# A fused retention, ELU and maxout kernel: the loads and the order of work of its first eight chunks

## The chip, the cores and the metric

The kernel runs on one core of one Trainium2 chip. The metric is the device time of one execution in microseconds (us), median over runs. TensorE (PE) multiplies matrices, VectorE (DVE) and ScalarE (ACT) work element by element, GpSimd (POOL) does a little, SyncE (SP) issues transfers. Each engine executes its own instructions in their written order and waits on semaphores for the others.

## The reference

Three layers stand one behind the other; only what matters is shown.

```
# 1 retention, B=4, H=8, S=768, D=64, gamma[h] = 1 - 2**(-5-h)
state = gamma * state + k[t] outer v[t];   y[t] = q[t] @ state / 8
x = y as (3072 tokens, 512)
# 2 ELU layer, d_ff = 2048
h = x @ w_in;  g = where(h > 0, h, exp(min(h, 0)) - 1);  x = g @ w_out
# 3 maxout layer, three experts of 768
h = max(x @ w1, x @ w2, x @ w3);  out = h @ w_out
```

The weights of layers 2 and 3 arrive in float64.

## The kernel before

Retention is worked in 24 chunks of 128 tokens (6 a batch entry). For a chunk `c`, `load(c)` brings 1 MB to a tile `x`: queries and keys transposed (L98 twice, the queries by halves; L100, the keys), then keys and values by token (L106). `scores` multiplies queries by keys on PE (L154, tile `sc`); `prep` scales the queries by `qdec` (DVE, tile `qd`) and the keys by a column of `cols` (ACT, 8 instructions at L136, tile `kd`), or both into a tile `spare` in an odd chunk; `mask` multiplies the scores by the decay table `dmask` (DVE, L166, tile `a`). `update` forms keys times values (PE, L182, tile `up`) and adds it to the decayed state (DVE, L189 and L192); `mix` makes the outputs from the old state (PE, L205) and from masked scores and values (PE, L209), both into `xo`, and casts them (ACT, L217, `xh`); `rest` keeps what the cast lost (DVE, L222, `xl`). The state makes this a chain over the chunks.

Four chunks are a block of 512 tokens for the ELU layer. `h1(b, f)` is 12 matmuls of block `b` with a 128-column piece `f` of `w_in` (L339), then exp, Relu, a max and a split on ACT and DVE (L346 to L352); `o1(b, f, ...)` is 12 matmuls with the same piece of `w_out` into four accumulators (L371); `x2_out` copies these out (L390, L392). Each product is made of three passes over high and low parts. A half of a piece's float64 words comes in by `load_half` (L244, tile `raw`, 512 KB, two buffers) and is turned into high and low float32 parts by `cv_bits`, `cv_rest`, `cv_high`, `cv_low`: six instructions on DVE and two on ACT; `cv_high` issues the load of the half after next.

PE, DVE, ACT and SP execute in the order in which the program is written. So the start of the program, up to the eight chunks, two `h1` and two `o1`, is an order made by hand: `begin(c)` is scores, prep, mask; `end(c)` is update, then mix. `junk(k)` is `k` matmuls on a tile of zeros. Behind that a loop over `(b, f)` runs one `h1` and one `o1` after the other with one conversion each, the later chunks between them, and a third part does the maxout layer.

Of the kernel before, what the change touches and what calls it, by code (L numbers as in the profile page):

```python
# [7 lines left out]
F32 = mybir.dt.float32  # L8
# [32 lines left out]
def kernel(ctx: ExitStack, tc: tile.TileContext, qkv0, qkv, wa, wb, dmask, qdec, cols, out):  # L41
# [8 lines left out]
    xpool = ctx.enter_context(tc.tile_pool(name="x", bufs=2))  # L50
    ps_acc = ctx.enter_context(tc.tile_pool(name="ps_acc", bufs=4, space=bass.MemoryType.PSUM))
    ps_h = ctx.enter_context(tc.tile_pool(name="ps_h", bufs=4, space=bass.MemoryType.PSUM))
    const = one.enter_context(tc.tile_pool(name="const", bufs=1))
    wpool = one.enter_context(tc.tile_pool(name="w", bufs=KFF - NRING))
    stage = one.enter_context(tc.tile_pool(name="stage", bufs=NSTAGE))
    ld = one.enter_context(tc.tile_pool(name="ld", bufs=2))
    at = one.enter_context(tc.tile_pool(name="at", bufs=1))
    dpool = one.enter_context(tc.tile_pool(name="dec", bufs=2))


    dmask_sb = const.tile([P, H, P], F32, name="dmask_sb")
    qdec_sb = const.tile([P, NPAIR, P], F32, name="qdec_sb")
    cols_sb = const.tile([P, 32], F32, name="cols_sb")[:, :H + NPAIR]
    state = [const.tile([P, NPAIR, D], F32, name=f"state{i}") for i in range(2)]
    x2d = dram.tile([KDM, P, NT], F32, name="x2d")
    kept = {(f, c): dram.tile([P, 2 * 512], F32, name=f"kept{f}_{c}") for f in range(RES, KFF) for c in range(2)}
    opd = [dram.tile([P, SETW], F32, name=f"opd{j}") for j in range(NE * KF2 // 2)]
# [10 lines left out]
    def load(c, part=None):  # L78


        if c >= NCHUNK:
            return

        early = c < EARLY
        src = qkv0 if early else qkv
        if part != 1:
            if c in raw_t:
                return
            if c < EARLY + 3:
                x = wpool.tile([P, NPAIR, 4, P], F32, tag="w", name="x")  # L90
            else:
                x = ld.tile([P, NPAIR, 4, P], F32, tag="r", name="x")
            raw_t[c] = x
            for r in range(2):
                h = slice(r * D, (r + 1) * D)
                for s in range(1 if early else 2):
                    cc = slice(s * 2 * P + r * P, s * 2 * P + (r + 1) * P)
                    nc.sync.dma_start(out=x[h, :, s, :], in_=src[c, :, h, cc].rearrange("p d t -> d p t"))  # L98
            if early:
                nc.sync.dma_start(  # L100
                    out=x[:, :, 1, :], in_=src[c, :, :, 2 * P:3 * P].rearrange("p t n -> t p n")
                )
        if part != 0:
            x = raw_t[c]
            o = 3 * P if early else 4 * P
            nc.sync.dma_start(  # L106
                out=x[:, :, 2:4, :].rearrange("t p s n -> t p (s n)"),
                in_=src[c, :, :, o:].rearrange("p t n -> t p n"),
            )
# [84 lines left out]
    def mix(c, pool, tag, then=None):  # L194
        v = raw_t[c][:, :, 3, :].rearrange("t p (r d) -> t p r d", r=2)
        qd = st_t[c][0]
        a = a_t.pop(c)
        xo = xo_t[c] = pool.tile([P, NPAIR, P], F32, tag=tag, name="xo")
        first = True
        if c % NCH != 0:  # L200
            old = state[1 - c % 2]
            for p in range(NPAIR):
                for r in range(2):
                    h = slice(r * D, (r + 1) * D)
                    nc.tensor.matmul(xo[h, p, :], old[h, p, :], qd[h, p, :], start=p == 0, stop=False)  # L205
            first = False
        for p in range(NPAIR):
            for r in range(2):
                nc.tensor.matmul(  # L209
                    xo[r * D:(r + 1) * D, p, :], v[:, p, r, :], a[:, r, p, :],  # L210
                    start=first and p == 0, stop=p == NPAIR - 1,
                )
        if then:
            then(c, pool, tag)
        del raw_t[c], st_t[c]
        b, t0 = divmod(c * P, BLK)
        nc.scalar.copy(x_t[b][0][:, :, t0:t0 + P], xo)  # L217

    def rest(c):
        b, t0 = divmod(c * P, BLK)  # L220
        xh, xl = x_t[b]
        nc.vector.tensor_tensor(  # L222
            out=xl[:, :, t0:t0 + P], in0=xo_t.pop(c), in1=f32(xh[:, :, t0:t0 + P]), op=ALU.subtract
        )
# [9 lines left out]
    def load_half(n):  # L234
        if n < len(keys):
            key = keys[n]
            if key[0] == "a":
                src, c = wa[key[1]], key[2]
            elif key[0] == "b":
                src, c = wb[2 * (2 * key[1] + key[3]) + key[2] // 2], key[2] % 2  # L240
            else:
                src, c = wb[2 * key[1] + 1], 1
            r = stage.tile([P, 512, 2], I32, tag="raw", name="raw")
            nc.sync.dma_start(  # L244
                out=r.rearrange("p n w -> p (n w)"), in_=src[:, c * 512:(c + 1) * 512].bitcast(I32)
            )
            half.append(r)
# [26 lines left out]
    def cv_bits(n):  # L274
        if n >= len(keys):
            return
        t = dpool.tile([P, 512], I32, tag="t", name="t")
        m = dpool.tile([P, 512], F32, tag="m", name="m")
        tmp[n] = (t, m)
        nc.vector.tensor_scalar(  # L280
            out=t, in0=half[n][:, :, 1], scalar1=0x7FFFFE00, scalar2=None, op0=ALU.bitwise_and
        )
        nc.scalar.activation(t, t, ACTF.Relu, scale=8.0, bias=-896.0 * 2 ** 23)  # L283

    def cv_rest(n):
        if n >= len(keys):
            return
        m = tmp[n][1]
        lo, hi = half[n][:, :, 0].bitcast(U32), half[n][:, :, 1]
        nc.vector.tensor_scalar(out=m.bitcast(I32), in0=hi, scalar1=0x1FF, scalar2=None, op0=ALU.bitwise_and)  # L290
        nc.vector.scalar_tensor_tensor(
            out=m, in0=lo, scalar=2.0 ** -32, in1=m.bitcast(I32), op0=ALU.mult, op1=ALU.add
        )
# [28 lines left out]
    def new_x(b):  # L322
        x_t[b] = (
            xpool.tile([P, KDM, BLK], F32R, tag="xh", name="xh"),
            xpool.tile([P, KDM, BLK], F32R, tag="xl", name="xl"),
        )
# [32 lines left out]
    def o1(b, f, f0, f1):  # L359
        g = g_t.pop((b, f))  # L360
        w = w_t[f, 1]
        if f == f0:
            acc_t[b] = [ps_acc.tile([P, BLK], F32, tag="acc", name="acc") for _ in range(KDM)]
        order = [[(1, 0), (0, 0)], [(0, 1)]]
        if fresh(b, f):
            order = [[p] for p in FRESH]
        first, final = order[0][0], order[-1][-1]
        for passes in order:
            for m in range(KDM):
                for p in passes:  # L370
                    nc.tensor.matmul(  # L371
                        acc_t[b][m], w[:, p[0], m * P:(m + 1) * P], g[p[1]],
                        start=f == f0 and p == first, stop=f == f1 - 1 and p == final,
                    )
# [125 lines left out]
    ctx.enter_context(tc.manual_schedule(engines={mybir.EngineType.SP}))  # L500
    ctx.enter_context(tc.manual_schedule(engines={mybir.EngineType.PE}))
    ctx.enter_context(tc.manual_schedule(engines={mybir.EngineType.DVE, mybir.EngineType.Activation}))
    load(0, 0)
    nc.sync.dma_start(out=cols_sb, in_=cols)
    nc.sync.dma_start(out=dmask_sb, in_=dmask)
    load(0, 1)
    load(1, 0)
    load(1, 1)
    nc.sync.dma_start(out=qdec_sb, in_=qdec)
    load(2)  # L510
    load(3)
    load_half(0)
    load_half(1)
    load(4)
    load(5)
    new_x(0)
    new_x(1)

# [4 lines left out]
    def junk(k):  # L523
        o = ps_h.tile([P, BLK], F32, tag="h", name="junk")
        for i in range(k):
            nc.tensor.matmul(o, zero[:, 0:P], zero, start=i == 0, stop=i == k - 1)  # L526

    def begin(c, pool=ps_h, tag="h"):
        scores(c, pool, tag)
        prep(c)  # L530
        mask(c)

    def end(c):
        update(c, ps_h, "h")
        mix(c, ps_h, "h")

    junk(15)
    begin(0, ps_acc, "acc")
    end(0)
    junk(12)  # L540
    rest(0)
    begin(1, ps_acc, "acc")
    for c in range(1, CB):
        if c + 1 < CB:
            begin(c + 1, ps_acc, "acc")
        end(c)
        if c < 3:
            rest(c)
            junk(5)
    cv_bits(0)  # L550
    cv_rest(0)
    rest(CB - 1)
    cv_high(0)
    load(6)
    cv_bits(1)
    cv_low(0)
    cv_rest(1)
    begin(4, ps_h, "h")
    h1(0, 0, [(cv_high, 1)])
    end(4)  # L560
    cv_low(1)
    begin(5, ps_h, "h")
    rest(4)
    o1(0, 0, 0, 2)
    cv_bits(2)
    cv_rest(2)
    end(5)
    cv_high(2)
    load(7)
    rest(5)  # L570
    cv_low(2)
    begin(6, ps_h, "h")
    h1(0, 1, [], [(cv_bits, 3)])
    end(6)
    begin(7, ps_h, "h")
    rest(6)
    cv_rest(3)
    cv_high(3)
    end(7)
    cv_low(3)  # L580
    o1(0, 1, 0, 2)
    cv_bits(4)
    rest(7)
    cv_rest(4)
    h1(1, 0, [(cv_high, 4)], [(cv_bits, 5)])
    x2_out(0, 0, 2, True)
    cv_low(4)
    cv_rest(5)
    n = 5
# [376 lines left out]
```

## Time and profile before

| | |
|---|---|
| median of 3 runs | 1018.7 us (1017.85 to 1019.39) |
| profiled execution, its own time | 1019.52 us |
| its span | 1017.7 us |
| PE busy | 999.9 us (98%) |
| DVE, ACT busy | 690.5 us (68%), 353.3 us (35%) |

The span is the profiled part of the execution; 1.8 us lie around it. Busy PE includes the zeros and matmuls that wait inside the pipeline. The mean granted clock of PE is 0.995 of full speed.

### The profile page before, as it was taken

The numbers are of one execution on the slowest core, as the hardware profiler recorded it, in microseconds if no ns is written. First come the engines' busy times: TensorE is split into PE (matmuls) and PEld (weight loads), VectorE is DVE, ScalarE is ACT, GpSimd is POOL, SyncE is SP. The second block draws the span as 40 slices with busy tenths as digits, with TensorE's granted clock in tenths as the row PEclk, the third lists the DMA queues.
The fourth block names the chain that finished last, engine by engine and source line by source line (L and its number), as shares of the span: only waits on it lengthen the run. The fifth ranks groups of instructions, "written<-read, shape, count | busy, mean of one in ns | idle before, by whom it ended". The sixth has DMA issues, their size and how long they took to land.

```text
span 1017.7 us, 14387 instructions
## 1 busy us (share of the span) xinstructions
PE 999.9 (98%) x5690; PEld 853.6 (84%) x5693; DVE 690.5 (68%) x1189; ACT 353.3 (35%) x629; POOL 33.9 (3%) x31
## 2 busy tenths in 40 slices
PE   8989999999999999999999999999999999999998
PEld 4767888877788877888888788899899989999996
DVE  3869888985576776677765653678648836874771
ACT  3446555532344444444434543411301221130110
POOL 0000000020000100000100000000000000000000
PEclk8999999999999999999999999999999999999999
DMA  9423236794736783677437725994246045304701
GB/s 282 139 87 121 86 106 206 228 289 150 231 116 196 233 296 113 210 269 272 133 131 282 255 105 189 373 354 190 83 179 225 1 147 209 130 11 145 268 1 62
DMA packets 75315, 180.78 MB, mean 178 GB/s; under 512 B 5872, under 2 KB 42736, under 8 KB 71024
## 3 DMA queue, kind: packets, MB, share of 16 engines
q1 hardware_dynamic: 73520, 176.71, 50.5%
q10 hardware_dynamic: 1728, 3.15, 0.8%
q8 instruction: 45, 0.74, 0.3%
q14 instruction: 22, 0.18, 0.1%
HBM read 139.20 MB, written 40.63 MB: 177 GB/s over the span
## 4 chain that ended last, share of the span: by engine, by line
PE 91%; DVE 5%; ACT 2%; DMA 1%; issue 1%; SPq 0%; DVEq 0%; ACTq 0%
PE pp L682 26%; PE hp L339 25%; PE acc L371 24%; PE ac L734 9%; PE xo L209 2%; PE sc L154 2%; PE xo L205 2%; PE up L182 1%; DVE gl L352 1%; DVE e L348 1%; DMA x<-in_qkv 1%; PE junk L526 1%; DVE t L298 1%; ACT gh L349 0%; DVE part L388 0%
## 5 line engine op out<-in xcount | busy, mean ns | idle before, releaser
L682 PE MATMUL pp<-xs,op 128*128 128x384 f32 x1512 | 267.8, 334 | 0.0
L682 PEld LDWEIGHTS pp<-xs,op 128*128 128x128 f32 x1512 | 263.3, 188 | 3.0
L339 PE MATMUL hp<-xh,w 128*128 128x512 f32 x768 | 250.6, 397 | 4.4 <-DVE state L192 2.3
L371 PE MATMUL acc<-gh,w 128*128 128x512 f32 x768 | 196.3, 394 | 2.3 <-DVE part L392 1.7
L339 PEld LDWEIGHTS hp<-xh,w 128*128 128x128 f32 x768 | 143.9, 188 | 39.7 <-ACT w L301 2.5
L371 PEld LDWEIGHTS acc<-gh,w 128*128 128x128 f32 x768 | 143.5, 188 | 37.1 <-issue 2.4
L348 DVE SCALAR_TENSOR_TENSOR e<-e,hp 128x512 f32<-128x512 f32 x96 | 65.8, 685 | 124.1 <-ACT e L347 124.1
L339 PE MATMUL hp<-xl,w 128*128 128x512 f32 x384 | 143.2, 393 | 0.0
L734 PE MATMUL ac<-w,g 128*128 128x512 f32 x432 | 104.5, 391 | 0.0
L371 PE MATMUL acc<-gl,w 128*128 128x512 f32 x384 | 104.2, 393 | 0.0
L346 ACT ACTIVATE e<-hp 128x512 f32<-128x512 f32 x96 | 57.3, 597 | 117.3 <-PE hp L339 117.3
L734 PEld LDWEIGHTS ac<-w,g 128*128 128x128 f32 x432 | 80.6, 188 | 14.9
L349 ACT CAST gh<-e 128x512 fp32r<-128x512 f32 x96 | 59.6, 621 | 85.5 <-DVE e L348 85.5
L698 ACT COPY u<-pp 128x384 f32<-128x384 f32 x36 | 17.3, 480 | 201.5 <-PE pp L682 127.5
L371 PEld LDWEIGHTS acc<-gl,w 128*128 128x128 f32 x384 | 72.2, 188 | 16.4
L339 PEld LDWEIGHTS hp<-xl,w 128*128 128x128 f32 x384 | 72.3, 188 | 15.5
L352 DVE TENSOR_TENSOR gl<-e,gh 128x512 fp32r<-128x512 f32 x96 | 68.8, 717 | 19.6 <-ACT gh L349 16.9
L690 DVE TENSOR_TENSOR c<-pp,u 128x384 f32<-128x384 f32 x96 | 52.9, 553 | 36.4 <-PE pp L682 35.8
L347 ACT ACTIVATE e<-e 128x512 f32<-128x512 f32 x96 | 60.7, 632 | 3.1
L283 ACT ACTIVATE t<-t 128x512 int32<-128x512 int32 x56 | 35.4, 633 | 50.3 <-DVE t L280 50.3
L301 ACT CAST w<-t 128x512 fp32r<-128x512 f32 x56 | 34.8, 621 | 40.2 <-DVE t L298 38.6
L712 DVE TENSOR_TENSOR h<-h,c 128x768 f32<-128x768 f32 x48 | 45.9, 957 | 1.6
(70 smaller groups left out, 825.6 us busy)
## 6 DMA issues: line engine op xcount, KB each, us to landing
op<-opd SPq DMA_DIRECT2D x24, 1792.0 KB, 7.4
w<-kept SPq DMA_DIRECT2D x56, 512.0 KB, 6.0
raw<-in_wa SPq DMA_DIRECT2D x32, 512.0 KB, 3.7
x<-in_qkv SPq DMA_DIRECT2D x24, 512.0 KB, 6.0
raw<-in_wb SPq DMA_DIRECT2D x24, 512.0 KB, 4.3
x<-in_qkv SPq DMA_DIRECT2D x80, 128.0 KB, 4.8
opd<-w SPq DMA_DIRECT2D x9, 1024.0 KB, 6.9
kept<-w SPq DMA_DIRECT2D x14, 512.0 KB, 5.1
```

Source lines behind the costliest of these rows:

```text
L283: nc.scalar.activation(t, t, ACTF.Relu, scale=8.0, bias=-896.0 * 2 ** 23)
L339: nc.tensor.matmul(hp, w[:, pw, kk * P:(kk + 1) * P], x[px][:, kk, :], start=k == 0, stop=k == len(order) - 1,)
L346: nc.scalar.activation(e, hp, ACTF.Exp)
L347: nc.scalar.activation(e, e, ACTF.Relu, scale=-1.0, bias=1.0)
L348: nc.vector.scalar_tensor_tensor(out=e, in0=e, scalar=-1.0, in1=hp, op0=ALU.mult, op1=ALU.max)
L349: nc.scalar.copy(gh, e)
L352: nc.vector.tensor_tensor(out=gl, in0=e, in1=f32(gh), op=ALU.subtract)
L371: nc.tensor.matmul(acc_t[b][m], w[:, p[0], m * P:(m + 1) * P], g[p[1]], start=f == f0 and p == first, stop=f == f1 - 1 and p == final,)
L682: nc.tensor.matmul(o, ws[i][:, pw, kk * P:(kk + 1) * P], xs[i][:, px, kk, :], start=k == 0, stop=k == 5)
L690: nc.vector.tensor_tensor(out=out, in0=a, in1=c, op=ALU.add)
L712: nc.vector.tensor_tensor(out=h_t[s, p][i], in0=h_t[s, p][i], in1=c[i], op=ALU.max)
L734: nc.tensor.matmul(ac_t[s, m], g[:, px, m * P:(m + 1) * P], wo_t[f][:, pw, :], start=first and i == 0, stop=final and i == 2,)
```

## The change

The three tables (`cols`, `dmask`, `qdec`) are issued from ACT's queue and no longer from SP's, with one small `Exp` between them, in front of which the table load of ACT now stands. SP issues all eight early chunks without a pause, with the first two weight halves behind chunks 2 and 3; chunks 6 and 7 were issued behind `cv_high(0)` and `cv_high(2)`. `finish(c)` is mix, then update. In the first four chunks the scores of the next chunk come before the mix of this one, and in chunks 5 to 7 `prep` stands ahead of `scores`. The zeros go from 15, 12, 5 and 5 to 15, 10 and 4. `cv_bits(0)` and `cv_rest(0)` stand between the chunks. `x2_out` of the first group stands ahead of the next `h1`. The pool `const` is allocated behind the other pools, and `cols_sb` has 12 columns.

```diff
@@ pools
-    const = one.enter_context(tc.tile_pool(name="const", bufs=1))
     wpool = one.enter_context(tc.tile_pool(name="w", bufs=KFF - NRING))
...
     dpool = one.enter_context(tc.tile_pool(name="dec", bufs=2))
+    const = one.enter_context(tc.tile_pool(name="const", bufs=1))
-    cols_sb = const.tile([P, 32], F32, name="cols_sb")[:, :H + NPAIR]
+    cols_sb = const.tile([P, H + NPAIR], F32, name="cols_sb")
@@ start
-    load(0, 0)
-    nc.sync.dma_start(out=cols_sb, in_=cols)
-    nc.sync.dma_start(out=dmask_sb, in_=dmask)
-    load(0, 1)
-    load(1, 0)
-    load(1, 1)
-    nc.sync.dma_start(out=qdec_sb, in_=qdec)
+    warm = dpool.tile([P, 1], F32, tag="m", name="warm")
+    nc.vector.memset(warm, 0.0)
+    nc.scalar.dma_start(out=cols_sb, in_=cols)
+    nc.scalar.dma_start(out=dmask_sb, in_=dmask)
+    nc.scalar.activation(warm, warm, ACTF.Exp)
+    nc.scalar.dma_start(out=qdec_sb, in_=qdec)
+    load(0)
+    load(1)
     load(2)
+    load_half(0)
     load(3)
-    load_half(0)
     load_half(1)
     load(4)
     load(5)
+    load(6)
+    load(7)
+    def finish(c):
+        mix(c, ps_h, "h", update)
+
     junk(15)
     begin(0, ps_acc, "acc")
-    end(0)
-    junk(12)
+    junk(10)
+    begin(1, ps_acc, "acc")
+    finish(0)
     rest(0)
-    begin(1, ps_acc, "acc")
-    for c in range(1, CB):
-        if c + 1 < CB:
-            begin(c + 1, ps_acc, "acc")
-        end(c)
-        if c < 3:
-            rest(c)
-            junk(5)
+    junk(4)
+    begin(2, ps_acc, "acc")
+    finish(1)
+    rest(1)
     cv_bits(0)
+    begin(3, ps_acc, "acc")
+    finish(2)
+    rest(2)
     cv_rest(0)
-    rest(CB - 1)
     cv_high(0)
-    load(6)
+    finish(3)
+    rest(3)
     cv_bits(1)
...
     h1(0, 0, [(cv_high, 1)])
-    end(4)
+    prep(5)
+    finish(4)
     cv_low(1)
-    begin(5, ps_h, "h")
+    scores(5, ps_h, "h")
+    mask(5)
     rest(4)
+    prep(6)
     o1(0, 0, 0, 2)
...
     h1(0, 1, [], [(cv_bits, 3)])
-    end(6)
-    begin(7, ps_h, "h")
+    finish(6)
+    scores(7, ps_h, "h")
+    mask(7)
...
     o1(0, 1, 0, 2)
+    rest(7)
     cv_bits(4)
-    rest(7)
+    x2_out(0, 0, 2, True)
     cv_rest(4)
     h1(1, 0, [(cv_high, 4)], [(cv_bits, 5)])
-    x2_out(0, 0, 2, True)
```

On SP, at the start of the program, the queue of before reads so (`x_131`, `x_138`, `x_144` are chunks 0 to 2; `raw_424` is the third weight half, `x_426` chunk 6):

```order
L100 DMA x_131<-in_qkv0 128x4x128
L504 DMA cols_sb_92<-in_cols 128x12
L505 DMA dmask_sb_90<-in_dmask 128x1024
L106 DMA x_131<-in_qkv0 128x4x256
L98 DMA x_138<-in_qkv0 64x4x128 x2
L100 DMA x_138<-in_qkv0 128x4x128
L106 DMA x_138<-in_qkv0 128x4x256
L509 DMA qdec_sb_91<-in_qdec 128x512
...
L244 DMA raw_424<-in_wa 128x1024
L98 DMA x_426<-in_qkv0 64x4x128 x2
```

Of the change it reads (`x_137` is chunk 0, `x_147` chunk 2, `x_154` chunk 3, `x_176` chunk 7; `raw_152` and `raw_398` are the first and the third weight half):

```order
L100 DMA x_137<-in_qkv0 128x4x128
L106 DMA x_137<-in_qkv0 128x4x256
L98 DMA x_142<-in_qkv0 64x4x128 x2
...
L106 DMA x_147<-in_qkv0 128x4x256
L244 DMA raw_152<-in_wa 128x1024
L98 DMA x_154<-in_qkv0 64x4x128 x2
L100 DMA x_154<-in_qkv0 128x4x128
...
L106 DMA x_176<-in_qkv0 128x4x256
L244 DMA raw_398<-in_wa 128x1024
```

The tables have left the queue, the first weight half has moved ahead of chunk 3, and the third one has moved behind chunks 6 and 7.

On PE, chunks 1 to 3 stand so in before (`spare` is an odd chunk, `kd`, `qd` and `a` an even one; zeros left out):

```order
L154 MATMUL sc<-x 128x128 x16
L182 MATMUL up<-x,spare 64x64 x8
L205 MATMUL xo<-spare,state_93 64x128 x8
L209 MATMUL xo<-spare,x 64x128 x8
...
L154 MATMUL sc<-x 128x128 x8
L182 MATMUL up<-x,kd 64x64 x8
L205 MATMUL xo<-qd,state_94 64x128 x8
L209 MATMUL xo<-a,x 64x128 x8
```

and so in the change:

```order
L154 MATMUL sc<-x 128x128 x8
L205 MATMUL xo<-spare,state_92 64x128 x8
L209 MATMUL xo<-spare,x 64x128 x8
L182 MATMUL up<-x,spare 64x64 x8
L154 MATMUL sc<-x 128x128 x8
L205 MATMUL xo<-qd,state_93 64x128 x8
L209 MATMUL xo<-a,x 64x128 x8
L182 MATMUL up<-x,kd 64x64 x8
```

The state's products have moved behind the two products of the output, and between chunks 1 and 3 no zeros are left.

On DVE, behind the second `o1`, before:

```order
L280 TENSOR_SCALAR t<-raw 128x512
L222 TENSOR_TENSOR xl<-xo,xh 128x4x128
L290 TENSOR_SCALAR m<-raw 128x512
L291 SCALAR_TENSOR_TENSOR m<-raw,m 128x512
L348 SCALAR_TENSOR_TENSOR e<-e,hp 128x512
L298 SCALAR_TENSOR_TENSOR t<-raw,t 128x512
L352 TENSOR_TENSOR gl<-e,gh 128x512
L280 TENSOR_SCALAR t<-raw 128x512
L392 COPY part<-acc 128x512 x2
```

and in the change:

```order
L222 TENSOR_TENSOR xl<-xo,xh 128x4x128
L280 TENSOR_SCALAR t<-raw 128x512
L392 COPY part<-acc 128x512 x2
L290 TENSOR_SCALAR m<-raw 128x512
L291 SCALAR_TENSOR_TENSOR m<-raw,m 128x512
L348 SCALAR_TENSOR_TENSOR e<-e,hp 128x512
```

The copies of the accumulators have moved ahead of the whole elementwise work of `h1(1, 0)`. Behind the places that the diff touches, the order of every engine is the same as before.

## Rows read from the trace of the kernel before

**Rows 1.** Busy time by stretch: us of each engine, granted clock, DMA share, GB/s.

```profile
8.65:35.40 26.75, 21.44 (x260) 16.09 (x263) 14.64 (x28) 12.59 (x40) 0.00 (x0) 0.87 0.84 245
35.40:62.40 27.00, 24.02 (x244) 19.29 (x244) 23.16 (x43) 14.57 (x39) 0.00 (x0) 0.94 0.50 150
62.40:84.60 22.20, 20.07 (x87) 15.56 (x85) 15.90 (x30) 11.12 (x20) 0.00 (x0) 1.00 0.23 81
84.60:200.00 115.40, 115.40 (x495) 92.92 (x496) 103.09 (x187) 65.50 (x108) 2.35 (x2) 1.00 0.45 147
```

**Rows 2.** Chain that ended last, in order of time: start, us, what.

```profile
3.85 6.34 DMA x<-in_qkv
...
10.26 1.28 ACT L136
...
35.39 3.06 PE hp L339 x12
...
62.48 2.99 PE acc L371 x12
...
84.58 3.06 PE acc L371 x12
```

**Rows 3.** Who waited for whom, PE, first 104 us: total, times, longest.

```profile
PE acc L371 <- DVE part L392: 1.7, 1, 1.7
```

**Rows 4.** Busy time by stretch, as in Rows 1, two answers.

```profile
1.75:3.50 1.75, 1.75 (x6) 0.60 (x4) 0.00 (x0) 0.00 (x0) 0.00 (x0) 1.00 0.43 123
3.50:5.25 1.75, 1.75 (x6) 0.60 (x4) 0.00 (x0) 0.00 (x0) 0.00 (x0) 1.00 0.96 217
...
0.00:10.20 10.20, 7.43 (x31) 3.06 (x31) 1.56 (x3) 0.00 (x0) 0.20 (x4) 1.00 0.72 203
10.20:17.70 7.50, 5.41 (x37) 4.20 (x39) 1.66 (x3) 5.16 (x16) 0.00 (x0) 0.54 1.15 316
17.70:30.40 12.70, 12.60 (x173) 9.07 (x174) 8.08 (x16) 5.64 (x21) 0.00 (x0) 1.00 0.95 294
```

**Rows 5.** Timeline of SP's queue: start, us, line, operation, tiles.

```profile
2.83 0.50 SPq L504 DMA_DIRECT2D cols_sb<-in_cols  x1
3.37 0.43 SPq L505 DMA_DIRECT2D dmask_sb<-in_dmask  x1
...
48.59 1.26 SPq L98 DMA_DIRECT2D x<-in_qkv  x2
```

**Rows 6.** Chain that ended last, the steps of chunk 2 on PE.

```profile
25.13 1.09 PE sc L154 x16
26.22 0.61 PE up L182 x16
26.84 1.02 PE xo L205 x16
27.86 1.02 PE xo L209 x16
```

**Rows 7.** Timeline, DVE, and ACT behind the second `h1`: start, us, line, operation, tiles.

```profile
27.98 0.42 DVE L192 TENSOR_TENSOR state<-up,state 128x256 f32<-128x256 f32 x1
...
46.09 0.41 DVE L280 TENSOR_SCALAR t<-raw 128x512 int32<-128x512 int32 x1
...
51.96 0.60 ACT L346 ACTIVATE e<-hp 128x512 f32<-128x512 f32 x1 [1.22 <-PE hp L339]
...
53.98 0.62 ACT L349 CAST gh<-e 128x512 fp32r<-128x512 f32 x1 [0.75 <-DVE e L348]
```

**Rows 8.** Busy time by stretch, as in Rows 1: around PE's lower clock.

```profile
12.00:17.40 5.40, 5.07 (x35) 3.99 (x37) 1.36 (x3) 3.13 (x13) 0.00 (x0) 0.50 1.17 303
17.40:35.40 18.00, 16.33 (x226) 12.06 (x226) 11.99 (x24) 7.74 (x26) 0.00 (x0) 1.00 0.69 211
...
51.90:57.10 5.20, 2.77 (x50) 2.37 (x49) 3.16 (x6) 3.26 (x7) 0.00 (x0) 1.00 0.53 165
57.10:62.40 5.30, 5.30 (x48) 4.46 (x48) 5.03 (x11) 2.23 (x8) 0.00 (x0) 0.68 0.21 60
```

More of the change, by code (lines that the diff above doesn't have):

```diff
@@ L566 @@
     cv_rest(2)
-    end(5)
+    finish(5)
     cv_high(2)
-    load(7)
     rest(5)
     cv_low(2)
-    begin(6, ps_h, "h")
+    prep(7)
+    scores(6, ps_h, "h")
+    mask(6)
     h1(0, 1, [], [(cv_bits, 3)])
-    end(6)
-    begin(7, ps_h, "h")
+    finish(6)
+    scores(7, ps_h, "h")
+    mask(7)
     rest(6)
@@ L578 @@
     cv_high(3)
-    end(7)
+    finish(7)
     cv_low(3)
     o1(0, 1, 0, 2)
+    rest(7)
     cv_bits(4)
-    rest(7)
+    x2_out(0, 0, 2, True)
     cv_rest(4)
     h1(1, 0, [(cv_high, 4)], [(cv_bits, 5)])
-    x2_out(0, 0, 2, True)
     cv_low(4)
```

## The prediction

> **What bounds the kernel now.** I read the busy time by stretch first. From 84.6 us on PE has no idle time: 115.40 of 115.40 us up to 200, DVE 103.09 [rows 1]. The diff ends before that point and leaves the order behind it alone, so what the change is worth is how much earlier PE comes to this state, which is the `o1` that the chain of waits starts at 84.58 [rows 2]. Three stretches lie ahead of it, each with a limit of its own. Up to the first `h1` (35.39) nobody is full: from 8.65 on DVE is busy for 14.64 of 26.75 us, PE for 21.44 with its zeros; one waits for the other along the chain of the chunks. From there to the second `o1` (62.48) DVE is close to its limit, 23.16 of 27.00. From 62.40 to 84.60 PE is busy for 20.07 of 22.20, so 2.13 us are all that can be had there [rows 1, 2].
>
> **First stretch, to the start of the first `h1`, now 35.39.** The tables leave SP's queue: their issues cost SP 0.50 and 0.43 us ahead of the second half of chunk 0, which lands at 10.19 (3.85 and 6.34) [rows 2, 5]. On ACT the three issues, the table load (1.28 us, between 10.26 and the first `kd`) and the tiny `Exp` cost nothing as long as chunk 0 lands later than they end: four things of 0.4 to 1.3 us, begun with the program, are over by 4 us. Without that cover they would cost these 3 us. The one-column memset on DVE delays the first zeros by a tenth; the scores of chunk 0 come behind 15 zeros as before, and `kd` of chunk 0 waits for its load.
>
> The load stream sets the rest. It moved 203 GB/s up to 10.20, 316 up to 17.70 and 294 up to 30.40 [rows 4]: 2.07 + 2.37 = 4.44 MB by 17.7. In the new order, ahead of and with the queries and keys of chunk 3, come the tables (0.79 MB), chunks 0 to 2 (1.05 each), the first weight half (0.52) and half of chunk 3 (0.52): 4.98 MB. At the old pace these have moved by 17.7 + 0.54/0.294 = 19.5 us. A transfer completes later than its own bytes by count, since later ones are in flight beside it: at 10.2, 2.07 MB had moved, and what had to be there is 1.57; 0.5 MB more are 1.7 us, so 21.2. Now the start: the first slices ran at 123 and 217 GB/s [rows 4] while SP was still issuing. Against 316 that is (0.193 + 0.099) x 1.75 = 0.51 MB, or 1.7 us, the most that a second queue can recover; the least is the 0.93 us of issue time. Queries and keys of chunk 3 land between 19.5 and 20.3; I take 19.9, and 21.2 as the bound if nothing is recovered. [...]
>
> Behind that landing PE's order is: scores of 3, the two output products and the update of 2, the two products and the update of 3, scores of 4, `h1`. Steps at full clock: 1.09 scores, 1.02 and 1.02 output, 0.61 update [rows 6]; one round is 3.74. Between the rounds lies the addition to the state, 0.42 [rows 7], with some 0.2, an estimate, for the last product to drain. Together 3.74 + 0.6 + 3.74 = 8.1, so `h1` starts at 28.0. Masks, casts and the first conversion lie beside it: from 8.65 on DVE had 14.64 us of work for the same stretch [rows 1], and from 8.65 to 28.0 there are 19.3. Term: 35.39 - 28.0 = **7.4 us**; 8 at the early landing, 6.1 at 21.2.
>
> **Second stretch, to the second `o1`, now 27.1 us long.** The same DVE instructions stand in it, 23.16 us of work [rows 1]; what they must still wait for is the second `h1`'s way through ACT, 0.60 for exp, as much for the Relu of the same shape and 0.62 for the cast [rows 7], 1.8 together. That makes 25.0. What goes: chunk 7's load, issued only at 48.59 [rows 5], is now there; its `kd` is made ahead of exp; and PE's lower clock from 57.10 to 62.40 (mean 0.68 [rows 8]) no longer stretches the chunk's products. Term: 27.1 - 25.0 = **2.1 us**, between 0.5 (if half of the other waits come back) and 2.5.
>
> **Third stretch, to the `o1` now at 84.58.** PE waited once for 1.7 us for DVE's copies of the accumulators [rows 3]; they now stand ahead of the work of the next `h1`, so that wait goes. Of the 2.13 us idle [rows 1] the rest was a wait for DVE, and DVE gets nearer, since PE gained more than it: 15.90 us of work, with waits for exp that stay. I give half back: **1.1 us**, between 0.4 and 2.1.
>
> The pool moved behind the others changes addresses, and with them which old tile a late load waits for; the order of all rows there is the same, so I cost it at nothing. It would cost only if a load became late for PE.
>
> **Sum:** 7.4 + 2.1 + 1.1 = 10.6 us. Against the profiled execution's own 1019.52 that gives 1008.9; it lies 0.8 above the median of the runs shown, so the predicted median is 1018.7 - 10.6 = 1008.1.
>
> **The rivals.** *The loads become the bound.* The third weight half now queues behind chunks 6 and 7: 10.75 MB through it, 2.58 more than the 8.17 that had moved by 30.4, so 8.8 us later by 294 GB/s: 39.2, less 0.9 to 1.7. DVE took it up at 46.09, 10.7 behind the start of `h1` [rows 7], which is 38.7 now. That is a tie, and with the half MB in flight it can be 1.5 us late; with chunk 3 at 21.2 also, the sum falls by 1.3 + 1.5 to 7.8: 1010.9. [...] Against it: from 35.40 to 62.40 only 150 GB/s were moved [rows 1], so nothing piles up behind it.
>
> *PE's clock falls in the head.* It fell after PE had worked 2.77 of 5.20 us (51.9 to 57.1), and stood at 0.50 from 12.0 to 17.4 behind an idle stretch; with 16.33 busy of 18.0 it kept 1.00 [rows 8]. Eight zeros are gone. By the steps above PE works about 15 of 17 us from the scores of chunk 1 to `h1`, so I think that it holds. One such fall of some 5 us doubles about 3 us of products, of which most lies on the chain: 2.5 us lost, 1010.6. [...]
>
> [...]
>
> *Nothing comes of it,* because a later wait takes back what the head gave, within 2 us of 1018.7. Against it: PE without idle time behind 84.6 [rows 1].
>
> **How the numbers follow.** Forecast (a gain of 8.7 to 12.6, its own range 1006.1 to 1010.0) 0.60; loads 0.20; a clock fall 0.13; slower 0.03; nothing 0.04. The likeliest is 1008.1. The low end is the sum of the upper bounds, 8.0 + 2.5 + 2.1 = 12.6: 1006.1. The high end takes in a clock fall on top of three quarters of the loads' 2.8: 10.6 - 2.1 - 2.5 = 6.0, 1012.7. Beyond these lie some 0.14. A measurement of this kernel can tell about 0.2%, 2 us, from no change: faster 0.93, same 0.04, slower 0.03.
>
> **What would show it.** In the new profile: `dmask` and `cols` on another queue and the second half of chunk 0 landed by 9.5; the table load over before 4 us; the first `h1` at 27.4 to 28.8; DVE without a wait for a `raw` at about 38; the second `o1` near 53; no wait of 1.7 for `part`; the steady `o1` at 74 instead of 84.58, and PE full from there. I am wrong if PE's granted clock shows 0.50 after chunk 0, if the third weight half lands behind 40 us, or if PE shows new idle time behind 90 us.

## The result, and the profile after

The changed kernel takes **1005.2 us** (median of 4 runs, 1003.86 to 1005.39) against 1018.57 of before; the ratio is 0.9866, 95% interval 0.9849 to 0.9883. The forecast was 1008.1 with a range from 1006.1 to 1012.7: the direction was right, and the gain of 13.4 us is larger than the 10.6 forecast, so that the time lies 0.9 below the low end. The profiled execution has its own time of 1005.29 and a span of 1003.5.

The chain of the changed kernel that ended last, in order of time (start, us, what), to be held against [rows 2]:

```profile
1.15 5.30 DMA dmask_sb<-in_dmask
...
7.33 6.80 DMA x<-in_qkv
...
14.15 8.86 DMA x<-in_qkv
...
23.09 2.02 ACT spare L136 x8
...
34.25 7.28 DMA raw<-in_wa
...
41.55 0.43 DVE t L280
...
76.43 3.03 PE acc L371 x12
79.47 2.72 PE hp L339 x12
82.19 2.72 PE acc L371 x12
```

Up to 23 us the chain is now a chain of loads, where before it was one of products. At 41.55 a load stands in it again: the third weight half. The steady `o1` starts at 76.43 in place of 84.58, so 8.15 us are gained there. But the span is 14.2 us shorter. Some 6 us came behind the point at which, by the forecast, nothing changes any more.

The busy time by stretch of the changed kernel, columns as in [rows 1], cut at its own first `h1`, second `o1` and steady `o1`:

```profile
8.65:29.15 20.50, 17.86 (x269) 14.19 (x268) 13.60 (x26) 11.22 (x38) 0.00 (x0) 1.00 1.14 302
29.15:55.60 26.45, 22.23 (x245) 17.61 (x245) 22.62 (x42) 14.70 (x40) 0.00 (x0) 1.00 0.54 147
55.60:76.40 20.80, 19.90 (x84) 15.52 (x84) 17.38 (x33) 11.00 (x20) 0.00 (x0) 1.00 0.30 102
76.40:190.00 113.60, 113.57 (x501) 94.03 (x502) 103.99 (x187) 65.57 (x108) 2.82 (x2) 1.00 0.46 149
```

The granted clock is 1.00 in every stretch (0.87 and 0.94 before, [rows 1]). PE is full from 76.40 on, as it was from 84.60 on. So the further gain cannot be idle time: the same matmuls must have become shorter.

PE's timeline of the changed kernel (start, us, line, operation, tiles, idle time before and its releaser) shows the scores of chunks 0 and 3, then the first `h1`:

```profile
8.41 1.16 PE L154 MATMUL sc<-x 64*128 64x128 f32 x16 [2.22 <-DMA x<-in_qkv]
...
20.80 1.16 PE L154 MATMUL sc<-x 64*128 64x128 f32 x16 [1.29 <-DMA x<-in_qkv]
...
29.16 1.19 PE L339 MATMUL hp<-xh,w 128*128 128x512 f32 x4 [0.47 <-ACT xh L217]
```

DVE's timeline shows two waits for weights:

```profile
41.55 0.43 DVE L280 TENSOR_SCALAR t<-raw 128x512 int32<-128x512 int32 x1 [1.16 <-DMA raw<-in_wa]
...
196.13 0.43 DVE L280 TENSOR_SCALAR t<-raw 128x512 int32<-128x512 int32 x1 [1.57 <-DMA raw<-in_wa]
```

In the middle of the steady part, the chain of the kernel before reads

```profile
135.23 2.80 PE acc L371 x12
138.03 2.80 PE hp L339 x12
```

and that of the changed kernel

```profile
136.59 2.72 PE acc L371 x12
139.31 2.72 PE hp L339 x12
```

The same twelve matmuls, on the same shapes and at the same granted clock of 1.00, take 2.72 in place of 2.80 us, 0.16 us less for each pair of `h1` and `o1`. In the kernel before this concerns only the pieces whose weights lie in the pool `w`; those in the ring had 2.72 already:

```profile
625.22 2.72 PE acc L371 x12
627.94 2.72 PE hp L339 x12
```

The gain grows with the pairs from `w`: 8.2 us at the start of `h1(0, 2)`, 10.7 at `h1(0, 10)`, 9.9 at `h1(2, 0)`, 14.3 at `h1(5, 15)`. Only the fall between 166 and 243 us goes the other way, and there stands the wait of 1.57 us above.

**The theory** (A): what the forecast costed at nothing, the pool moved behind the others, moved the start of `w` from 0 to 128 modulo 256 bytes (by the allocation of the built program). `xh`, `xl`, the tiles of `g` and the ring lie at 128 in both. The address changes the time of a matmul, and the new loads and order of the head gain what was forecast. **Rivals**: (B) the head gains it all, through some later effect; (C) it is the place of the pool, not its residue (called D in the expectations of `front_pad128` and `after_pad128`).

### The profile page after: what moved, and what is told of

It is laid out like the page before. It is cut to its first block, busy times and chain, and to the rows that moved or that the text cites. A ratio compares the mean times of both kernels' runs of the same rounds, so it can differ in the third digit from the quotient of the medians.

```text
span 1003.5 us, 14377 instructions
## 1 busy us (share of the span) xinstructions
PE 984.8 (98%) x5684; PEld 848.0 (85%) x5685; DVE 690.7 (69%) x1190; ACT 352.9 (35%) x630; POOL 35.9 (4%) x31
## 4 chain that ended last, share of the span: by engine, by line
PE 86%; DVE 7%; DMA 4%; ACT 2%; issue 1%; SPq 0%; ACTq 0%; DVEq 0%
PE pp L693 26%; PE hp L339 24%; PE acc L371 23%; PE ac L745 10%; DMA x<-in_qkv 2%; DMA raw<-in_wa 1%; PE xo L209 1%; PE sc L154 1%; PE xo L205 1%; DVE gl L352 1%; DVE e L348 1%; DVE part L388 1%; DVE t L298 1%; ACT gh L349 1%; DVE w L307 1%; DVE m L291 1%
## 5 line engine op out<-in xcount | busy, mean ns | idle before, releaser
L339 PE MATMUL hp<-xh,w 128*128 128x512 f32 x768 | 248.1, 394 | 4.7 <-DVE state L192 2.5
L371 PE MATMUL acc<-gh,w 128*128 128x512 f32 x768 | 193.9, 391 | 3.1 <-ACT w L301 1.7
L339 PEld LDWEIGHTS hp<-xh,w 128*128 128x128 f32 x768 | 143.7, 188 | 38.1 <-ACT w L301 2.4
L339 PE MATMUL hp<-xl,w 128*128 128x512 f32 x384 | 141.9, 390 | 0.0
L339 PEld LDWEIGHTS hp<-xl,w 128*128 128x128 f32 x384 | 72.1, 188 | 14.4
L283 ACT ACTIVATE t<-t 128x512 int32<-128x512 int32 x56 | 35.4, 633 | 54.1 <-DVE t L280 54.1
```

Of the source, the lines that this page charges most:

```text
L339: nc.tensor.matmul(hp, w[:, pw, kk * P:(kk + 1) * P], x[px][:, kk, :], start=k == 0, stop=k == len(order) - 1,)
L371: nc.tensor.matmul(acc_t[b][m], w[:, p[0], m * P:(m + 1) * P], g[p[1]], start=f == f0 and p == first, stop=f == f1 - 1 and p == final,)
```

## Experiments: which edit gains what

All times are medians of 4 or 5 runs, beside runs of the kernel before on the same chip (1019.05, 1018.95 and 1018.59 in three sets; the ratios are against these); positions are starts of the first weight load in one trace. The expectations go by the median distance of weight loads: 227 ns where twelve matmuls take 2.72 us, 230 to 232 where they take 2.80.

**pools_only** takes the kernel before with this one edit, and **head_only** the changed kernel without it.

```diff
-    const = one.enter_context(tc.tile_pool(name="const", bufs=1))
     wpool = one.enter_context(tc.tile_pool(name="w", bufs=KFF - NRING))
...
     dpool = one.enter_context(tc.tile_pool(name="dec", bufs=2))
+    const = one.enter_context(tc.tile_pool(name="const", bufs=1))
```

> The kernel before with one line moved: the pool of constants behind the others, nothing else, so the weight tiles of the ELU layer begin 0x2080 bytes lower, at 128 instead of 256 modulo 512. Theory A (two separate gains, the order at the start 8 us and the address of the weight tiles 6 us): matmuls of h1 and o1 with pieces 0 to 8 go from a median spacing of 230 to 232 ns to 227, as pieces 13 to 15 have it already; time 1012.5 us, between 1011 and 1013.5. Rival B (all 13.4 us come of the order at the start, and the closer spacing follows from it): 1018.6 and spacing as before. Rival C (the place of the constants costs DVE or ACT, not PE): faster, but the spacing of PE stays at 230 to 232.

> The changed kernel with the pool of constants and the 32 columns put back as before: the whole order at the start, the old addresses. Theory A: the gain stops at what the start gives, 8 us at the first steady o1 (76.4 as in the changed kernel, at most 1 us later), spacing 230 to 232 with pieces 0 to 8; time 1010.5, between 1009.5 and 1011.5. Rival B: 1005.2, spacing 227.

`pools_only`: 1010.68, ratio 0.9916 (0.9901 to 0.9931). `head_only`: 1008.8, ratio 0.9897 (0.9883 to 0.9912). B falls: the pool alone gains 8.4 us and leaves the first `h1` where it was (35.63), with 2.72 us for twelve matmuls from `w`. The head alone gains 10.3 us, close to the forecast. Its timeline on PE has the scores of chunk 3 and the first `h1` earlier than the changed kernel:

```profile
19.27 1.16 PE L154 MATMUL sc<-x 64*128 64x128 f32 x16 [0.52 <-DMA x<-in_qkv]
...
27.68 1.20 PE L339 MATMUL hp<-xh,w 128*128 128x512 f32 x4 [0.51 <-ACT xh L217]
```

Its gain is 10.7 us at the steady `o1` and 10.6 at the last `h1`: flat, as the forecast had it. The two edits together give less than their sum, so the pool also costs something in the head.

**front_pad128** is the kernel before with 64 in place of 32 columns for `cols_sb`; the pool stays in front, and `w` starts at 128. **after_pad128** is the changed kernel with 128 B ahead of `w`, which then starts at 0.

```diff
-    cols_sb = const.tile([P, 32], F32, name="cols_sb")[:, :H + NPAIR]
+    cols_sb = const.tile([P, 64], F32, name="cols_sb")[:, :H + NPAIR]
```

```diff
+    pad = one.enter_context(tc.tile_pool(name="pad", bufs=1))
     wpool = one.enter_context(tc.tile_pool(name="w", bufs=KFF - NRING))
...
-    warm = dpool.tile([P, 1], F32, tag="m", name="warm")
+    warm = pad.tile([P, 32], F32, name="warm")[:, :1]
```

> The kernel before with cols_sb 64 instead of 32 columns wide: the constants stay in front and grow by 128 bytes, so the weight tiles begin 128 bytes higher, at 384 modulo 512. Theory A in the form that the address modulo 256 decides (128 good, 0 bad): as pools_only, 1012.5. Rival D (the place in the memory decides: how far the weights lie from the other operand, or what lies in front of them): 1018.6.

> The changed kernel with 128 unused bytes ahead of the weight pool, so its tiles begin at 256 modulo 512 and the constants stay behind all pools. Theory A, address modulo 256: the addresses' part is lost, 1010.5 to 1011.5, spacing 230 to 232 with pieces 0 to 8. Rival D: 1005.2, spacing 227.

1010.74 (ratio 0.9919, 0.9904 to 0.9934) and 1009.98 (0.9911, 0.9895 to 0.9928). C falls: 128 B gain 8 us without any pool being moved, and 128 B take 5 us from the changed kernel. All four runs ended faster than theory A's figures for them, by 0.3 to 1.8 us.

**after_all128** puts the same pad ahead of the ring, the first pool, so that all pools start at 0. **before_all128** does this to the kernel before, with `cols_sb` as the pad. **after_pad64** has 16 columns in the pad ahead of `w`, which then starts at 192. **after_pad_stage** has the pad of 128 B between `w` and `stage`, so that `raw` and all behind it move and `w` stays.

```diff
+    pad = ctx.enter_context(tc.tile_pool(name="pad", bufs=1))
     ring = ctx.enter_context(tc.tile_pool(name="ring", bufs=NRING))
```

> The changed kernel with 128 B of padding ahead of every pool, so that all tiles lie at 0 modulo 256: the weights in `w` as in the kernel before, and the ring, `xh`, `xl` and `g` there too, which lay at 128 in every kernel so far. Theory A1, it is the address of the tiles by itself that sets 227 or 231 ns between matmuls: all pieces run at 231, those of the ring too (34 pairs of `h1` and `o1` more, 0.16 us each, 5.4 us), on top of the 1010.0 that padding `w` alone gave: 1015 or more, later still if the maxout part slows too. Theory A2, what counts is whether both operands of a matmul share the residue: 227 everywhere, with the faster loads that padding `w` had shown in the first 27 us (first h1 near 27.7 in place of 29.16): 1002 to 1003.

> The kernel before, with `cols` moved to the front so that the ring, `xh`, `xl` and `g` lie at 0 modulo 256 as `w` does; order, loads and the place of the early chunks as before. Theory S (operands of one residue): spacing 227 in all pieces, head as in before or up to 1.3 us earlier, as padding had shown: 1010.0 to 1011.5. With the head alone at 1008.8 this would then add up: 1018.6 less 7 to 8 and less 10 is 1000.6 to 1002, where the changed kernel with all pools at 0 had 1002.2. Rival, the two effects don't add up because pushing PE makes another engine or the loads the bound: 1008 or lower here.

> The changed kernel with 64 B of padding ahead of `w`: weights and early chunks lie at 192 modulo 256, `xh`, `xl`, `g` and the ring at 128 as before. Theory S, both operands of a matmul have to share the residue modulo 256: spacing of the pieces in `w` above 227 (231 if any difference counts alike), end near 1010 with faster loads, 1011 to 1012 without. Rival, only the difference of 128 counts and 64 is harmless: 227 everywhere, 1003 to 1005.5. For the loads: if 128 modulo 256 is the only slow place, the first h1 starts near 27.7; if any place but 0 is slow, near 29.2 or later.

> The changed kernel with 128 B of padding between `w` and the pools behind it: weights and early chunks stay at 128 modulo 256, `raw` and all behind it move to 0. Theory R, it was the residue of `raw` that made the loads of the first 27 us slower (303 in place of 331 GB/s): most of the 2.5 us at the head come back, first h1 near 28, 1002.5 to 1003.5. Theory X, it was the residue of the early chunks in `w`: head as in the changed kernel, first h1 29.2; at most the wait for `raw` of 1.57 us near 196 us shrinks: 1004 to 1005.2. Matmul spacing 227 by both.

What came out, with the residues modulo 256, the GB/s of the stretch 8.65 to 27 us, and what the chain shows in its middle for twelve matmuls from `w`:

| kernel | early chunks and `w` | `raw` | `xh`, `xl`, `g` | twelve matmuls | GB/s | first `h1` | median |
|---|---|---|---|---|---|---|---|
| before | 0 | 0 | 128 | 2.80 | 326 | 35.39 | 1018.57 |
| pools_only | 128 | 128 | 128 | 2.72 | 298 | 35.63 | 1010.68 |
| front_pad128 | 128 | 128 | 128 | 2.72 | 294 | 34.57 | 1010.74 |
| before_all128 | 0 | 0 | 0 | 2.72 | 317 | 35.51 | 1010.64 |
| head_only | 0 | 0 | 128 | 2.79 | 331 | 27.68 | 1008.8 |
| after_pad128 | 0 | 0 | 128 | 2.80 | 329 | 28.08 | 1009.98 |
| after | 128 | 128 | 128 | 2.72 | 303 | 29.16 | 1005.2 |
| after_pad_stage | 128 | 0 | 128 | 2.72 | 304 | 29.17 | 1004.58 |
| after_pad64 | 192 | 192 | 128 | 2.80 | 278 | 31.23 | 1015.69 |
| after_all128 | 0 | 0 | 0 | 2.72 | 336 | 27.33 | 1002.16 |

The ratios of the last four experiments: `before_all128` 0.9922 (0.9907 to 0.9936), `after_pad64` 0.9970 (0.9957 to 0.9984), `after_all128` 0.9836 (0.9820 to 0.9851), `after_pad_stage` 0.9865 (0.9845 to 0.9885; its four runs spread from 1002.57 to 1006.32, so by time it can't be told from the changed kernel, and its trace is of the fastest).

Two things are to be read from the table. First, the time of twelve matmuls goes by the **difference** of two addresses and not by either: with `w` at 0 they take 2.80 us beside `xh` at 128 and 2.72 beside `xh` at 0, with `w` at 128 they take 2.72 beside 128, and a difference of 64 has 2.80 as one of 128 has. That 256 is the modulus goes by two kernels: `w` is at 128 modulo 512 in `pools_only` and at 384 in `front_pad128`, and both have 2.72. The chain of `after_pad64` and that of `after_all128` (a line of code was added, so L339 is L340):

```profile
138.57 2.80 PE hp L340 x12
```

```profile
138.97 2.72 PE acc L372 x12
```

Second, the loads go by the address of the early chunks **by itself**: 317 to 336 GB/s at 0, 294 to 304 at 128, 278 at 192, whatever the rest does. The stretches of `after_all128` and of `after_pad64`, columns as above:

```profile
8.65:27.00 18.35, 16.89 (x257) 13.35 (x254) 13.50 (x25) 11.06 (x38) 0.00 (x0) 1.00 1.13 336
```

```profile
8.65:27.00 18.35, 15.10 (x215) 11.89 (x218) 10.52 (x19) 9.57 (x35) 0.00 (x0) 1.00 1.16 278
```

`after_pad64` ended later than expected by either theory: with the same time per matmul as `after_pad128` it is 5.2 us behind it at `h1(1, 2)` already (69.78 and 64.55), so nearly all of the 5.7 us between the two medians comes of the slower loads. The DMA engines are busy in both stretches, at 1.13 and 1.16, and move 278 GB/s at 192 where they move 336 at 0. Why the rate goes by the address was not shown.

`after_pad_stage` separates the two kinds of loads: the first `h1` stays at 29.17, so for it the address of the chunks counts and not that of `raw`. But the third weight half came in 1.0 us earlier, and so did the second `o1` (54.62 in place of 55.59).

The two effects don't quite add up: 8.20 us (`before_all128`) and 10.62 (`head_only`) at the last `h1` against 17.43 for both (`after_all128`). At `h1(0, 10)` nothing is missing (2.84 and 11.07 against 13.78). The missing 1.4 us lie between `h1(0, 10)` and `h1(2, 0)`, where DVE waits for `raw` in `after_all128` too (1.60 us at 192.9).

What this wait costs can be read across the traces, one of each kernel. On the way from `h1(0, 10)` to `h1(2, 0)`, four kernels with 2.72 us gain 0.8 us more on the kernel before, and DVE does not wait for `raw` there (`front_pad128`, `before_all128`, `after_pad_stage`, `after_old_order`). Four others lose 0.6 to 0.9 us, and there it waits for 1.5 to 1.9 us (the changed kernel, `after_all128`, `after_third`, `after_tables_sp`); only in these does PE then stand idle for 0.7 to 1.1 us until ACT has done its part of the conversion (L283). So the wait takes about 1.5 us. Why some have it is open. It is not that PE comes earlier: `after_pad_stage` starts `h1(0, 10)` at 165.13 and has no such wait, `after_tables_sp` at 168.57 and waits for 1.9 us.

## Experiments: the parts of the head

**after_tables_sp** issues the tables from SP's queue again, at the places they had before, and **after_third** issues chunk 7 behind the third weight half.

```diff
-    nc.scalar.dma_start(out=cols_sb, in_=cols)
-    nc.scalar.dma_start(out=dmask_sb, in_=dmask)
     nc.scalar.activation(warm, warm, ACTF.Exp)
-    nc.scalar.dma_start(out=qdec_sb, in_=qdec)
-    load(0)
+    load(0, 0)
+    nc.sync.dma_start(out=cols_sb, in_=cols)
+    nc.sync.dma_start(out=dmask_sb, in_=dmask)
+    load(0, 1)
     load(1)
+    nc.sync.dma_start(out=qdec_sb, in_=qdec)
```

```diff
     load(6)
-    load(7)
...
     cv_high(0)
+    load(7)
     finish(3)
```

> The changed kernel with the three tables issued from SP's queue at the places of the kernel before. By the forecast's step the second queue recovers up to 1.7 us of loads: chunk 3 lands 1.0 to 1.3 us later and so does the first h1 (30.2 to 30.5): 1006.2 to 1006.5. Rival, dmask's large packets got ahead of chunk 0's queries on the other queue, so nothing was recovered: first h1 at 29.2 or earlier, 1004.5 to 1005.2.

> The changed kernel with chunk 7 issued behind the third weight half. Theory L, the loads have become the bound there: the half lands at about 41.5 - 1.05 MB / 0.3 = 38.0, the wait of 1.16 us on DVE goes, the second o1 starts about 1 us earlier (54.5), and the time is 1004.0 to 1004.5. Rival, the wait is made up for by later idle time anyway, or chunk 7 becomes late in its place: 1005.2 or up to 1006.

`after_tables_sp`: 1007.26, ratio 0.9886 (0.9870 to 0.9903, which overlaps with the changed kernel's), first `h1` at 32.86, 3.7 us later, of which 2.5 are left at the steady `o1`. The issue of `qdec` on SP's timeline

```profile
7.06 2.87 SPq L511 DMA_DIRECT2D qdec_sb<-in_qdec  x1
```

holds up all loads behind it: that of chunk 2 is issued at 9.97 in place of 7.33. On PE's timeline the scores of chunk 0 and of chunk 1 read

```profile
6.79 1.16 PE L154 MATMUL sc<-x 64*128 64x128 f32 x16
...
13.50 2.08 PE L154 MATMUL sc<-x 64*128 64x128 f32 x16 [3.28 <-DMA x<-in_qkv]
```

In the changed kernel they start at 8.41 and 11.86. So the expectation's rival is right for chunk 0, which comes 1.6 us earlier when `dmask` stands behind it in one queue; but chunk 1 comes 1.6 us later. Its scores follow an idle stretch of 3.28 us and take 2.08 us, where they take 1.16 in the changed kernel; the granted clock of the stretch is 0.72:

```profile
8.00:20.00 12.00, 8.50 (x63) 5.84 (x64) 4.77 (x8) 4.62 (x17) 0.00 (x0) 0.72 1.14 293
```

From the scores of chunk 1 to those of chunk 2 it takes 6.29 us in place of 3.89, and PE waits for no load on the way. The scores of chunk 3, which wait for their load in both kernels, start at 23.77 in place of 20.80. So the second queue is worth more than the 1.0 to 1.3 us expected: it brings chunk 3 some 3.0 us forward, and it keeps PE from the idle stretch ahead of the lower clock. How much of the 3.7 us at the first `h1` is the queue and how much the clock was not separated.

`after_third`: 1003.68, ratio 0.9850 (0.9833 to 0.9866). DVE takes up the third half without a wait:

```profile
40.59 0.42 DVE L280 TENSOR_SCALAR t<-raw 128x512 int32<-128x512 int32 x1
```

The second `o1` starts 1.0 us earlier, and 1.3 us are left at the last `h1`. The wait of 1.16 us was a real loss; the time alone would not tell it (the intervals overlap).

**after_old_order** puts the PE order of before back into chunks 0 to 3 (`end(c)` for `finish(c)`, and `begin(1, ...)` behind `rest(0)`), and **after_zeros** the zeros of before.

```diff
     begin(0, ps_acc, "acc")
+    end(0)
     junk(10)
+    rest(0)
     begin(1, ps_acc, "acc")
-    finish(0)
-    rest(0)
     junk(4)
     begin(2, ps_acc, "acc")
-    finish(1)
+    end(1)
...
```

```diff
-    junk(10)
+    junk(12)
...
-    junk(4)
+    junk(5)
...
     rest(1)
+    junk(5)
```

> The changed kernel with the order of before on PE in chunks 0 to 3: the state's products ahead of the output's, and the scores of chunk 1 behind chunk 0's outputs; loads, tables, zeros and addresses as changed. By the forecast's steps the landing of chunk 3 sets the first h1 and the products behind it are the same 3.74 us a round in either order, so the order is worth nothing or little: first h1 29.2 to 29.7, 1005.2 to 1005.8. Rival, the order is what gained: with the outputs behind the update the casts of the last chunk come later, first h1 at 30.5 or later, 1006.5 or more.

> The changed kernel with the zeros of before, 12, 5 and 5 in place of 10, 4 and none. PE waits for loads in the head anyway, so by the forecast the eight zeros lie beside these waits: first h1 29.2, 1005.2. Rival, they stand in front of products that are ready, at 0.22 us each: five behind chunk 1 alone cost 1.1, first h1 at 30.3 or later, 1006.3 to 1007.

`after_old_order`: 1004.92, ratio 0.9869 (0.9853 to 0.9886); the first `h1` at 30.34 is 1.2 us later, the second `o1` only 0.3. `after_zeros`: 1005.06, ratio 0.9866 (0.9851 to 0.9880); 0.7 us later at both. Neither can be told from the changed kernel by its time, and by the last `h1` both are even ahead (1.4 and 0.6 us), through the stretch around 200 us, where DVE waits for `raw` not at all in the one and for 0.7 us in the other. So of the head's gain the loads give most; this is by what is left, since the new order on SP and the new places of `prep` and `x2_out` were not taken back one by one. The order of the products gives 1.2 us at the first `h1` that the next wait takes back, and fewer zeros 0.7. The rival of the order, 30.5 or later, was near at the first `h1` and fell at the end.

## Why the prediction was wrong, point by point

| term | forecast | head_only | after |
|---|---|---|---|
| first stretch | 7.4 | 7.7 | 6.2 |
| second stretch | 2.1 | 1.8 | 0.6 |
| third stretch | 1.1 | 1.2 | 1.3 |
| behind the steady `o1` | 0 | -0.1 | 6.1 |
| sum | 10.6 | 10.6 | 14.3 |

The columns are differences of positions: the first `h1`, the second `o1`, the steady `o1` and the last `h1`, 35.39, 62.41, 84.58 and 643.87 before, 27.68, 52.90, 73.88 and 633.25 in `head_only`, 29.16, 55.59, 76.43 and 629.61 after.

**The step that failed** is "The pool moved behind the others changes addresses [...] so I cost it at nothing". It looked at which old tile a load waits for, and not at what an address does to a transfer or a matmul. What the runs showed in its place: it was worth about 8 us behind the steady `o1` where nothing else stood in the way (`before_all128`, 8.20 less 0.25), because twelve matmuls from `w` took 2.72 in place of 2.80 us. Of these the changed kernel kept 6.1; most of the rest went with DVE's wait of 1.57 us for `raw` at 196 us. In the head the same step cost 2.5 us (`head_only` is that much earlier at the steady `o1`).

**First stretch.** The mechanism was right in the main. Queries and keys of chunk 3 were put at 19.5 to 20.3 and 8.1 us of products behind them. With the address of before they let the scores start at 19.27, and `h1` follows 8.41 later. With the moved address it is 20.80 and 8.36. What the 8.1 left out is the wait of 0.47 us for the cast `xh` ahead of `h1`, which the forecast put beside the products. The 0.6 between the rounds, of which 0.2 for the last product was an estimate without a row, is 0.55 in the changed kernel: so long PE stands idle, until the addition to the state (L192) releases the output products that start at 25.03. The table load was over at 2.9 us, as costed. Not foreseen was that `dmask` on the second queue gets ahead of chunk 0: it lands at 6.45, and the scores of chunk 0 wait 2.22 us for queries and start at 8.41 (6.79 with the tables on SP), and the second half of chunk 0 landed at 10.19, where "by 9.5" was forecast; the wait for chunk 3 hides both. The second queue itself was put too low, at 0.93 to 1.7 us for the landing of chunk 3, where `after_tables_sp` shows 3.0: the sum has the issues of `cols` and `dmask` and leaves out that of `qdec`, which stands ahead of chunk 2 and took 1.79 us in the trace of the kernel before. If that holds at the old address too, an estimate, the scores of chunk 3 would have started there at 19.27 + 3.0 = 22.3 without the second queue, behind the 21.2 forecast for that case; so that 7.4 and 7.7 lie so close is in part luck.

**Second stretch.** The rival that the loads become the bound came true in part. The third weight half landed at 41.5, and the forecast's sign of it was "behind 40 us". The rival had priced this at 39.2 and half a megabyte in flight; the slower transfers (303 GB/s from 8.65 to 27.00, 331 in `head_only`) did the rest, for in `head_only`, with the same order of loads and the old addresses, DVE took the half up at 38.83 without a wait (38.7 by the forecast). It cost 1.0 us, as `after_third` shows, and in `head_only` the second `o1` came at 52.90, where "near 53" was forecast.

**Third stretch.** Right: PE's wait of 1.7 us for `part` [rows 3] does not occur any more.

**The clock** held at 1.00, as forecast. `after_tables_sp` shows how near the other case was: with the scores of chunk 1 at 13.50 in place of 11.86, and PE idle for 3.28 us ahead of them, the granted clock from 8.00 to 20.00 was 0.72. For a time slower than before, put at 0.03, no run stands: the slowest variant, `after_pad64`, took 1015.69 us.

A version beats both kernels: `after_all128`, 1002.16 us, with 128 B more of memory.

## What to carry to other kernels

A tile pool that is moved or padded changes start addresses, and these are work to be costed like any edit: compare the time of the same matmul group in two pools of one trace, which here had 2.80 and 2.72 us side by side before anything was changed. As far as these runs go (float32 operands, differences of 64 and 128), keep the operands of a matmul at one residue modulo 256 (2.72 us for twelve in place of 2.80), and the destinations of transfers in pieces of 512 B and 1 KB at a multiple of 256 (336 GB/s in place of 303 at 128 and 278 at 192). When a head is bound by loads, look first at what stands in the queue ahead of the needed tile; order and filling of the engine behind it gave little here (1.2 and 0.7 us at the first `h1`).

## What the runs showed of the hardware

- Twelve matmuls of 128x128 by 128x512 took 2.72 us when the weights' pool and the pools of the other operand started at the same residue modulo 256 (`pools_only`, `front_pad128`, `before_all128`, `after_all128`, after), and 2.80 when they differed by 64 (`after_pad64`) or 128 (before, `after_pad128`; 2.79 in `head_only`). Whether it is the weights or the other operand that comes later was not tried, and no difference below 64 was.
- From 8.65 to 27 us the loads moved 336, 303 and 278 GB/s in the same program with the tiles of the early chunks and of `raw` at 0, 128 and 192 modulo 256 (`after_all128`, after, `after_pad64`), and 304 with `raw` alone at 0 (`after_pad_stage`). The chunks come in pieces of 512 B and 1 KB, by their shapes; in the first 45 us of the changed kernel 13040 packets are under 2 KB and 752 of them under 512 B, and the 12288 between are just what eight chunks make of such pieces.
- A table of 512 KB on a second queue, issued at 1.15 us, landed at 6.45, while the queries and keys of chunk 0, another 512 KB issued between 0.74 and 2.77 on the first, let the scores start only at 8.41. With the table behind them on the first queue they started at 6.79 (`after_tables_sp`).
